# Part of the low-part work of layer one's gates on GpSimd, one gate kept in its PSUM bank, and the reserved bank also in layer two

## The chip, the cores and the metric

The kernel runs on one core of one Trainium2 chip. The metric is the device time of one execution in microseconds. The engines have short names in the profile: PE is TensorE (PEld its weight loads), DVE is VectorE, ACT is ScalarE, POOL is GpSimd, SP is SyncE. Times in the trace count from the start of the span.

## The reference, cut to what matters

A Fourier filter over the sequence comes first, then two feed-forward layers, all in float32:

```
y  = irfft(rfft(x) * (filt_r + 1j*filt_i))          # 2 x 3008 x 256 -> 6016 tokens x 256
h1 = y @ w_in                                       # 256 -> 2048
g1 = where(h1 > 0, h1, exp(min(h1, 0)) - 1)         # layer one: elu
z  = g1 @ w_out                                     # 2048 -> 256
h2 = z @ w2_in
out = (h2 * clip(h2 + 3, 0, 6) / 6) @ w2_out        # layer two
```

## The kernel before

Every matrix product of the two layers is done in three matmuls: operands are split into a high part (a rounded copy, made by ACT) and a low part (what is left, made by a subtraction). The three are weights-high by data-high, weights-low by data-high, weights-high by data-low (`mm3`, L88, L89 and L90). So the third matmul of each triple, L90, is the first to need the low part of the data.

The work of interest is that of **the groups**. The last four token blocks of layer one and all twelve of layer two are worked on in pairs, a pair being a round; layer one has two rounds, layer two six, and a round has eight groups, one for each two tiles of the hidden dimension. That makes 16 groups of layer one and 48 of layer two. A group takes a two-by-two block product with seven products instead of eight (`prod`, numbered 1 to 7, three matmuls each), which yields four hidden tiles, the keys (0,0), (1,1), (1,0) and (0,1). Of each hidden tile a gate value is made (`relu`, `exp`, `gate`), split (`high` on ACT at L674, `low` on DVE at L679), and multiplied with the output weights in the next group (`second`, two halves of three matmuls for each key). A group is thus 7 x 3 + 4 x 2 x 3 = 45 matmuls.

The order of the instructions on every engine is the order of the program's text. `elu_group` writes it out for layer one's groups and for the first group of layer two, `group` for the others. In them `old` is the group before, whose gates are finished and used, and `g` is the present one. In a layer-one group PE does prod 1, second (0,0), prod 2, 6, 5, second (1,1), prod 7, second (1,0), the first half of second (0,1), prod 4, the second half of second (0,1), prod 3. In the first group of layer two prod 2 stands ahead of second (0,0).

The gates of layer one need a minimum with zero, an exponential, and one scalar-tensor-tensor instruction on DVE (L666) that reads the exponential and the hidden tile h. For (0,0) h lies in a PSUM bank, for (1,0) too; for (1,1) and (0,1) it is a sum in SBUF (`add`, L634). Before, all four gates are written to SBUF, over the exponential.

At four places of a group, `slot(0)` to `slot(3)`, other work is put in: splits of the next round's operands (`x_high` L559 on ACT, `x_low` L564 on DVE; in groups 4 to 7 of a round `x_low` stands in `slot(1)`), the conversion of layer two's weights in small steps on ACT and DVE, and loads. POOL issues three kinds of loads in this stretch: `s0_load` (L384) and `s_load` (L389), the summed weights, and `w_load` (L457), layer two's weights. Each waits in POOL's queue until the buffer it fills is free. POOL has no arithmetic in these groups before.

PSUM has eight banks. Seven are handed out in turn (`bank()`, pool `ps`), one is reserved (`lone()`, pool `ps1`). A round keeps four banks for its outputs. A group takes three more for its products, a, b and c: prod 1, 6, 7 and 4 write to a, prod 2 to b, prod 5 and 3 to c. In layer one b is the reserved bank, and holds prod 1's result (copied by ACT, L750) before prod 2 is added to it; in layer two all three come from the seven.

Of the kernel before, what the change touches and what calls it, by code (L numbers as in the profile page):

```python
# [12 lines left out]
AF = mybir.ActivationFunctionType  # L13
ALU = mybir.AluOpType
# [28 lines left out]
def _f32(t):  # L43
    return t.bitcast(F32)
# [3 lines left out]
def fft_conv_moe_moe2(ctx, tc, xp, fq, sg, cs1, cs1t, cs2, ci2, ci1, ident, w1i, w1o, w2i, w2o, out):  # L48
    nc = tc.nc
# [11 lines left out]
    def name(s):  # L61
        uid[0] += 1
        return f"{s}_{uid[0]}"
# [4 lines left out]
    def t2(shape, dt=F32):  # L68
        return p2.tile(shape, dt, tag="t2", name=name("t2"))

    def bank():
        return ps.tile([P, 512], F32, tag="ps", name=name("ps"))

    def lone():
        return ps1.tile([P, 512], F32, tag="lone", name=name("lone"))
# [25 lines left out]
    def halves_of(t, k=2):  # L101
        return t.rearrange("p (a b) -> p a b", a=k)
# [4 lines left out]
    def like(t, n):  # L107
        return t[:, :n] if n == 512 else halves_of(t[:, :n])
# [171 lines left out]
    stt = nc.vector.scalar_tensor_tensor  # L280
# [9 lines left out]
    def w_words(layer, f):  # L290
        raw = raws.pop((layer, f))
        low, high = raw[:, :, 0], raw[:, :, 1]
        v, e, r = t2([P, 512]), t2([P, 512], U32), t2([P, 512])
        ahead[layer, f] = v, r
        nc.scalar.activation(v, _f32(high), AF.Abs)
        yield
        nc.vector.tensor_scalar_max(v, v, LEAST)
        nc.vector.tensor_scalar(
            e, v.bitcast(U32), 3, 0x3FFFFFFF, op0=ALU.logical_shift_left, op1=ALU.bitwise_and
        )  # L300
        yield
        stt(out=v.bitcast(U32), in0=high, scalar=0xC0000000, in1=e, op0=ALU.bitwise_and, op1=ALU.bitwise_or)
        yield
        nc.vector.tensor_scalar(e, v.bitcast(U32), 0xFF800000, None, op0=ALU.bitwise_and)
        yield
        stt(out=r, in0=low, scalar=2.0**-52, in1=_f32(e), op0=ALU.mult, op1=ALU.mult)
        yield
# [262 lines left out]
    def prod(l, p, q, m, acc, start):  # L570
        n = WIDTHS[l, p]
        if m in (1, 2):
            w = wts[l, 2 * q][:, :, (m - 1) * P : m * P]
        elif m == 4:
            w = wts[l, 2 * q + 1][:, :, P : 2 * P]
        else:
            w = sums[l, q][:, :, {5: 0, 6: 1, 7: 2, 3: 3}[m], :]
        x = ops[l, p, m]
        mm3(acc[:, :n], w[:, 0], w[:, 1], pairs(x[:, 0, :n]), pairs(x[:, 1, :n]), start, True, True)
# [40 lines left out]
    class Group:  # L620
# [39 lines left out]
        def gate(self, key):  # L660
            h, r = self.source(key), like(self.g[key], self.n)
            del self.h[key]
            if self.l:
                stt(out=r, in0=r, scalar=6.0, in1=h, op0=ALU.min, op1=ALU.mult)  # L664
            else:
                stt(out=r, in0=r, scalar=-1.0, in1=h, op0=ALU.add, op1=ALU.max)  # L666

        def part(self, key):
            self.high(key)
# [1 line left out]

        def high(self, key):
            g, gh = self.g[key], t2([P, 512], F32R)
            nc.scalar.activation(gh[:, : self.n], g[:, : self.n], AF.Copy)  # L674
            self.g[key] = g, gh

        def low(self, key):
            (g, gh), gl, n = self.g[key], t2([P, 512], F32R), self.n
            nc.vector.tensor_tensor(out=gl[:, :n], in0=g[:, :n], in1=_f32(gh[:, :n]), op=ALU.subtract)  # L679
            self.g[key] = gh, gl  # L680

        def second(self, key, d=(0, 1)):
# [7 lines left out]
    def group(l, p, q, old, first, beside):  # L690

        def slot(i):
            for fn in beside[i]:
                fn()

        g = Group(l, p, q)
        a, b, c = bank(), bank() if l else lone(), bank()
        if l == 0 or (old and old.l == 0):
            return elu_group(g, a, b, c, old, first, slot)
        prod(l, p, q, 1, a, True)  # L700
        m1 = g.copy(a)
        prod(l, p, q, 2, b, True)
        g.add((0, 0), m1, b)
        old.part((1, 0))
        old.relu((0, 1))
        old.gate((0, 1))
        old.second((0, 0))
        g.relu((0, 0))
        g.gate((0, 0))
        slot(0)  # L710
        prod(l, p, q, 6, a, False)
        u2 = g.copy(a)
        old.part((0, 1))
        slot(1)
        prod(l, p, q, 5, c, True)
        g.part((0, 0))
        slot(2)
        old.second((1, 1))
        prod(l, p, q, 7, a, False)
        u3 = g.copy(a)  # L720
        g.add((1, 1), u3, c)
        old.second((1, 0))
        old.finish(0)
        g.relu((1, 1))
        g.gate((1, 1))
        slot(3)
        old.second((0, 1), (0,))
        prod(l, p, q, 4, a, False)
        g.h[1, 0] = a
        g.relu((1, 0))  # L730
        if not g.last:
            g.gate((1, 0))
        old.second((0, 1), (1,))
        old.finish(1)
        if g.last:
            g.u2, g.c = u2, c
            return g
        g.part((1, 1))
        prod(l, p, q, 3, c, False)
        g.add((0, 1), u2, c)  # L740
        return g
# [268 lines left out]
    with tc.manual_schedule():  # L1010
# [27 lines left out]
        for step in PROLOGUE.split():  # L1038
            what, h, g = step[:-2], int(step[-2]), int(step[-1])
# [68 lines left out]
        n = place[0] = NU  # L1108
        for l, p in ROUNDS:
            for q in range(GROUPS):  # L1110
                old = group(l, p, q, old, [rest(NU + i) for i in range(3)], pre[n : n + 4])
                n += 4
# [98 lines left out]
```

## Time and profile before

| what | value |
|---|---|
| time, median of 3 runs | 1054.93 us (1054.42 to 1055.36) |
| the profiled execution | 1063.18 us, of which the span is 1061.4 us |
| PE busy | 1048.8 us, 99% of the span |
| DVE busy | 886.1 us, 83% |
| ACT busy | 797.7 us, 75% |
| POOL busy | 202.7 us, 19% |
| granted clock of TensorE | full in every slice |

The profiled execution is 8.25 us longer than the median of the runs. A matmul of 512 columns stands in the trace with 0.38 us, while the next one starts 0.22 us after it, since matmuls overlap; a stall of PE therefore shows as a longer step between two starts, and in the idle time before a weight load (PEld), with the engine whose semaphore ended it.

### The profile page before, as it was taken

The numbers are of one execution on the slowest core, as the hardware profiler recorded it, in microseconds if no ns is written. First come the engines' busy times: TensorE is split into PE (matmuls) and PEld (weight loads), VectorE is DVE, ScalarE is ACT, GpSimd is POOL, SyncE is SP. The second block draws the span as 40 slices with busy tenths as digits, with TensorE's granted clock in tenths as the row PEclk, the third lists the DMA queues.
The fourth block names the chain that finished last, engine by engine and source line by source line (L and its number), as shares of the span: only waits on it lengthen the run. The fifth ranks groups of instructions, "written<-read, shape, count | busy, mean of one in ns | idle before, by whom it ended". The sixth has DMA issues, their size and how long they took to land.

```text
span 1061.4 us, 14383 instructions
## 1 busy us (share of the span) xinstructions
PE 1048.8 (99%) x5022; PEld 918.7 (87%) x5022; DVE 886.1 (83%) x1427; ACT 797.7 (75%) x1437; POOL 202.7 (19%) x218
## 2 busy tenths in 40 slices
PE   9999999999999999999999999999999999999998
PEld 7688888888889989988888888888888888888998
DVE  2899999898886799889989978888888888888776
ACT  2478888897767888877877867777777777777766
POOL 1720000444546745300021100010010010000000
PEclk9999999999999999999999999999999999999999
DMA  9785100374645454610365710100100100100100
GB/s 278 246 263 198 50 16 1 106 222 151 196 135 178 153 193 152 213 55 6 133 236 161 231 73 21 60 1 21 60 14 27 40 18 18 41 1 1 40 1 35
DMA packets 57944, 107.31 MB, mean 101 GB/s; under 512 B 5008, under 2 KB 33680, under 8 KB 57872
## 3 DMA queue, kind: packets, MB, share of 16 engines
q1 hardware_dynamic: 52144, 88.21, 25.3%
q0 software_dynamic: 4896, 17.83, 5.4%
q8 instruction: 39, 0.64, 0.3%
q10 hardware_dynamic: 832, 0.36, 0.1%
q14 instruction: 33, 0.27, 0.1%
HBM read 69.42 MB, written 36.96 MB: 100 GB/s over the span
## 4 chain that ended last, share of the span: by engine, by line
PE 82%; ACT 7%; DVE 7%; issue 2%; DMA 2%; POOL 1%; SPq 0%; DVEq 0%; ACTq 0%; POOLq 0%
PE ps L90 24%; PE ps L88 24%; PE ps L89 24%; PE ps L158 2%; PE lone L88 1%; PE lone L90 1%; PE lone L89 1%; PE ps L245 1%; DVE t L85 1%; ACT t L84 1%; DMA scr<-t 1%; POOL t L217 1%; DVE t L679 1%; PE ps L202 1%; DVE t L634 1%
## 5 line engine op out<-in xcount | busy, mean ns | idle before, releaser
L88 PE MATMUL ps<-t,w 128*128 128x512 f32 (+1 forms) x1120 | 421.2, 376 | 2.3 <-DVE t L634 1.3
L90 PE MATMUL ps<-t,w 128*128 128x512 f32 (+1 forms) x1120 | 420.2, 375 | 0.7 <-DVE t L85 0.6
L89 PE MATMUL ps<-t,w 128*128 128x512 f32 (+1 forms) x1120 | 419.6, 375 | 0.2 <-DVE w L316 0.2
L88 PEld LDWEIGHTS ps<-t,w 128*128 128x128 f32 x1120 | 211.7, 189 | 29.4 <-DVE t L498 1.9
L90 PEld LDWEIGHTS ps<-t,w 128*128 128x128 f32 x1120 | 211.6, 189 | 28.4 <-DVE t L679 2.2
L89 PEld LDWEIGHTS ps<-t,w 128*128 128x128 f32 x1120 | 211.7, 189 | 25.9 <-DVE w L316 1.6
L679 DVE TENSOR_TENSOR t<-t,t 128x512 fp32r<-128x512 f32 (+1 forms) x256 | 175.7, 701 | 24.1 <-ACT t L674 22.5
L674 ACT ACTIVATE t<-t 128x512 fp32r<-128x512 f32 (+1 forms) x256 | 154.0, 616 | 6.1 <-DVE t L664 5.7
L628 ACT ACTIVATE t<-ps 128x512 f32<-128x512 f32 (+1 forms) x176 | 103.2, 586 | 64.9 <-PE ps L90 63.3
L634 DVE TENSOR_TENSOR t<-ps,t 128x512 f32<-128x512 f32 (+1 forms) x176 | 118.1, 679 | 14.2 <-ACT t L628 13.0
L664 DVE SCALAR_TENSOR_TENSOR t<-t,t 128x512 f32<-128x512 f32 (+1 forms) x144 | 97.6, 705 | 33.3 <-ACT t L648 32.7
L648 ACT ACTIVATE t<-t,three 128x512 f32<-128x512 f32 (+1 forms) x144 | 97.2, 707 | 37.3 <-DVE t L634 36.6
L495 ACT ACTIVATE t<-ps 128x512 f32<-128x512 f32 (+1 forms) x128 | 74.1, 579 | 30.1 <-PE ps L90 28.1
L84 ACT ACTIVATE t<-t 128x512 fp32r<-128x512 f32 (+2 forms) x108 | 66.2, 618 | 22.5 <-POOL t L217 20.0
L496 ACT ACTIVATE t<-t 128x512 f32<-128x512 f32 (+1 forms) x128 | 79.3, 619 | 4.1
L85 DVE TENSOR_TENSOR t<-t,t 128x512 fp32r<-128x512 f32 (+2 forms) x96 | 73.3, 769 | 10.6 <-ACT t L84 10.4
L548 POOL TENSOR_TENSOR t<-t,t 128x512 f32<-128x512 f32 (+1 forms) x12 | 16.2, 1351 | 286.0 <-DVE t L634 257.0
L498 DVE SCALAR_TENSOR_TENSOR ps<-t,ps 128x512 f32<-128x512 f32 (+1 forms) x76 | 50.4, 663 | 23.0 <-ACT t L496 22.5
L88 PE MATMUL ps<-t,t 128*128 128x512 f32 (+1 forms) x160 | 60.2, 376 | 0.6 <-DVE t L634 0.6
L89 PE MATMUL ps<-t,t 128*128 128x512 f32 (+1 forms) x160 | 60.1, 376 | 0.0
L90 PE MATMUL ps<-t,t 128*128 128x512 f32 (+1 forms) x160 | 60.1, 376 | 0.0
L85 DVE TENSOR_TENSOR t<-ps,t 128x512 fp32r<-128x512 f32 (+1 forms) x76 | 49.9, 656 | 0.1
(115 smaller groups left out, 1520.6 us busy)
## 6 DMA issues: line engine op xcount, KB each, us to landing
t<-in_fq SPq DMA_DIRECT2D x24, 512.0 KB, 6.2
scrw<-t SPq DMA_DIRECT2D x16, 512.0 KB, 2.8
w<-scrw POOLq DMA_DIRECT2D x16, 512.0 KB, 5.0
t<-in_xp SPq DMA_DIRECT2D x16, 384.0 KB, 6.0
scr<-t SPq DMA_DIRECT2D x24, 256.0 KB, 3.0
t<-scr SPq DMA_DIRECT2D x16, 384.0 KB, 5.2
scrx<-t SPq DMA_DIRECT2D x10, 512.0 KB, 3.3
t<-scr POOLq DMA_DIRECT2D x10, 512.0 KB, 6.1
```

The source lines that it names most:

```text
L84: nc.scalar.activation(hi, src, AF.Copy)
L85: eng.tensor_tensor(out=lo, in0=src, in1=_f32(hi), op=ALU.subtract)
L88: nc.tensor.matmul(acc, wh, xh, start=start, stop=False, skip_group_check=more)
L89: nc.tensor.matmul(acc, wl, xh, start=False, stop=False, skip_group_check=more)
L90: nc.tensor.matmul(acc, wh, xl, start=False, stop=stop, skip_group_check=more)
L496: nc.scalar.activation(t[:, :n], t[:, :n], AF.Exp, scale=-1.0)
L628: nc.scalar.activation(like(t, self.n), got(bank_, self.n), AF.Copy)
L634: nc.vector.tensor_tensor(out=like(self.h[key], n), in0=got(bank_, n), in1=like(u, n), op=ALU.add)
L648: nc.scalar.activation(like(r, n), h, AF.Relu, bias=three)
L664: stt(out=r, in0=r, scalar=6.0, in1=h, op0=ALU.min, op1=ALU.mult)
L674: nc.scalar.activation(gh[:, : self.n], g[:, : self.n], AF.Copy)
L679: nc.vector.tensor_tensor(out=gl[:, :n], in0=g[:, :n], in1=_f32(gh[:, :n]), op=ALU.subtract)
```

## The change

In layer one's groups the low parts of keys (0,0) and (0,1) are made by POOL and no longer by DVE. The gate of key (1,0) is written back to the PSUM bank that holds h, in place, and its high and low parts are then made from the bank, which is held until the low part is done. In layer two's groups b is the reserved bank, as in layer one. High and low parts are written through the same view as the gate, which changes nothing for blocks of 512 columns.

```
         def gate(self, key):
             h, r = self.source(key), like(self.g[key], self.n)
             del self.h[key]
             if self.l:
                 stt(out=r, in0=r, scalar=6.0, in1=h, op0=ALU.min, op1=ALU.mult)
+                self.g[key] = r
             else:
-                stt(out=r, in0=r, scalar=-1.0, in1=h, op0=ALU.add, op1=ALU.max)
+                g = h if key == (1, 0) else r
+                stt(out=g, in0=r, scalar=-1.0, in1=h, op0=ALU.add, op1=ALU.max)
+                self.g[key] = g
...
         def high(self, key):
             g, gh = self.g[key], t2([P, 512], F32R)
-            nc.scalar.activation(gh[:, : self.n], g[:, : self.n], AF.Copy)
+            nc.scalar.activation(like(gh, self.n), g, AF.Copy)
             self.g[key] = g, gh
 
         def low(self, key):
             (g, gh), gl, n = self.g[key], t2([P, 512], F32R), self.n
-            nc.vector.tensor_tensor(out=gl[:, :n], in0=g[:, :n], in1=_f32(gh[:, :n]), op=ALU.subtract)
+            eng = nc.gpsimd if not self.l and key in ((0, 0), (0, 1)) else nc.vector
+            eng.tensor_tensor(out=like(gl, n), in0=g, in1=_f32(like(gh, n)), op=ALU.subtract)
             self.g[key] = gh, gl
...
         g = Group(l, p, q)
-        a, b, c = bank(), bank() if l else lone(), bank()
+        a, b, c = bank(), lone(), bank()
```

## Rows read from the trace of the kernel before

**Rows 1.** Windows: length, busy of five engines (instructions), clock, DMA; layer one's groups, layer two's

```profile
436.00:517.00 81.00, 80.25 (x371) 68.96 (x370) 72.45 (x130) 63.43 (x118) 6.69 (x10) 1.00 0.27 89
597.00:677.00 80.00, 79.89 (x370) 69.64 (x370) 65.88 (x106) 57.96 (x100) 1.58 (x3) 1.00 0.22 72
```

**Rows 2.** Waits of PE's weight loads, 436 to 600 us: total, times, longest

```profile
PEld ps L88 <- DVE t L634: 2.8, 2, 1.7
PEld ps L90 <- DVE t L679: 2.0, 7, 0.5
PEld lone L88 <- ACT lone L750: 0.7, 2, 0.4
```

**Rows 3.** Timeline: start, duration, instruction, idle before; one late weight load, matmuls around it

```profile
482.09 0.19 PEld L90 LDWEIGHTS ps<-t,w 128*128 128x128 f32 x1 [0.22 <-DVE t L679]
...
482.11 0.47 PE L90 MATMUL ps<-t,w 128*128 128x512 f32 x1
482.42 0.38 PE L88 MATMUL ps<-t,w 128*128 128x512 f32 x1
```

**Rows 4.** Timeline of PE's weight loads at two starts of a round of layer two

```profile
595.64 0.19 PEld L88 LDWEIGHTS ps<-t,w 128*128 128x128 f32 x1 [1.71 <-DVE t L634]
...
673.72 0.19 PEld L88 LDWEIGHTS ps<-t,w 128*128 128x128 f32 x1 [0.51 <-DVE t L664]
```

**Rows 5.** Timeline of ACT in layer one's thirteenth group, which starts at 555.51

```profile
555.51 0.58 ACT L750 ACTIVATE lone<-ps 128x512 f32<-128x512 f32 x1 [1.32 <-PE ps L90]
...
558.11 0.60 ACT L628 ACTIVATE t<-ps 128x512 f32<-128x512 f32 x1
...
560.28 0.61 ACT L674 ACTIVATE t<-t 128x512 fp32r<-128x512 f32 x1
...
561.27 0.62 ACT L674 ACTIVATE t<-t 128x512 fp32r<-128x512 f32 x1
```

**Rows 6.** Timeline of DVE in the same group

```profile
561.01 0.68 DVE L679 TENSOR_TENSOR t<-t,t 128x512 fp32r<-128x512 f32 x1
561.61 0.68 DVE L564 TENSOR_TENSOR t<-t,t 128x512 fp32r<-128x512 f32 x1
```

**Rows 7.** Timeline of PE's weight loads in the same group

```profile
561.79 0.19 PEld L89 LDWEIGHTS ps<-t,w 128*128 128x128 f32 x1
562.01 0.19 PEld L90 LDWEIGHTS ps<-t,w 128*128 128x128 f32 x1
...
565.25 0.19 PEld L90 LDWEIGHTS ps<-t,w 128*128 128x128 f32 x1
```

**Rows 8.** Line 85, the same subtraction elsewhere: ns min/median/max, first and last start, shapes

```profile
L85 DVE TENSOR_TENSOR t<-t,t x96: 657/685/1774, 58.4 to 393.7; 128x512 fp32r<-128x512 f32 x76, 96x512 fp32r<-96x512 f32 x16, 128x448 fp32r<-128x448 f32 x4
...
L85 DVE TENSOR_TENSOR t<-ps,t x76: 610/677/727, 221.4 to 439.4; 128x512 fp32r<-128x512 f32 x44, 128x448 fp32r<-128x448 f32 x32
...
L85 POOL TENSOR_TENSOR t<-t,t x12: 1274/1279/1289, 235.8 to 309.6; 128x512 fp32r<-128x512 f32 x12
```

**Rows 9.** Timeline of POOL and DVE where their instructions overlap, two places

```profile
840.82 1.28 POOL L548 TENSOR_TENSOR t<-t,t 128x512 f32<-128x512 f32 x1 [47.11 <-DVE t L634]
...
840.91 1.74 DVE L679 TENSOR_TENSOR t<-t,t 128x512 fp32r<-128x512 f32 x1
...
428.53 0.69 DVE L564 TENSOR_TENSOR t<-t,t 128x512 fp32r<-128x512 f32 x1
...
428.58 1.78 POOL L330 TENSOR_TENSOR t<-t,t 128x512 fp32r<-128x512 f32 x1
```

**Rows 10.** Timeline of ACT and POOL: a high part, and POOL's low part of it

```profile
253.94 0.63 ACT L84 ACTIVATE t<-t 128x512 fp32r<-128x512 f32 x1
...
254.70 1.28 POOL L85 TENSOR_TENSOR t<-t,t 128x512 fp32r<-128x512 f32 x1 [1.96 <-issue]
```

**Rows 11.** Timeline of POOL's loads in layer one's groups

```profile
508.33 0.53 POOL L384 DMA_DIRECT2D t<-scr  x1 [44.19 <-PE lone L90]
...
581.68 0.53 POOL L457 DMA_DIRECT2D w<-scrw  x1 [7.24 <-PE ps L90]
```

More of the change, by code (lines that the diff above doesn't have):

```diff
@@ L664, in gate @@
                 stt(out=r, in0=r, scalar=6.0, in1=h, op0=ALU.min, op1=ALU.mult)
+                self.g[key] = r
             else:
-                stt(out=r, in0=r, scalar=-1.0, in1=h, op0=ALU.add, op1=ALU.max)
+                g = h if key == (1, 0) else r
+                stt(out=g, in0=r, scalar=-1.0, in1=h, op0=ALU.add, op1=ALU.max)
+                self.g[key] = g
         def part(self, key):
@@ L673, in high @@
             g, gh = self.g[key], t2([P, 512], F32R)
-            nc.scalar.activation(gh[:, : self.n], g[:, : self.n], AF.Copy)
+            nc.scalar.activation(like(gh, self.n), g, AF.Copy)
             self.g[key] = g, gh
@@ L678, in low @@
             (g, gh), gl, n = self.g[key], t2([P, 512], F32R), self.n
-            nc.vector.tensor_tensor(out=gl[:, :n], in0=g[:, :n], in1=_f32(gh[:, :n]), op=ALU.subtract)
+            eng = nc.gpsimd if not self.l and key in ((0, 0), (0, 1)) else nc.vector
+            eng.tensor_tensor(out=like(gl, n), in0=g, in1=_f32(like(gh, n)), op=ALU.subtract)
             self.g[key] = gh, gl
@@ L696, in group @@
         g = Group(l, p, q)
-        a, b, c = bank(), bank() if l else lone(), bank()
+        a, b, c = bank(), lone(), bank()
         if l == 0 or (old and old.l == 0):
```

## The prediction

> **What bounds the kernel now.** The page comes first: TensorE is busy for nearly the whole span (the table above), so no other engine can be worth more than the gaps in TensorE's stream. The windows come second, because the edits touch two stages [rows 1]. In both the granted clock is 1.00, TensorE's upper level, and TensorE starts a matmul about every 0.216 us (45 matmuls, a group, take 9.72 us); but VectorE is busy 72.45 of 81 us in layer one's groups and 65.88 of 80 us in layer two's. So layer one's groups run with VectorE close behind TensorE, and layer two's have room.
>
> The third view is the waits of TensorE's weight loads from 436 to 600 us [rows 2]: 2.0 us in seven waits for a low part (L679), 2.8 us in two for a sum (L634), 0.7 us in two for the copy into the reserved bank. A weight load normally runs ahead of its matmul, so a wait costs less than it shows. The late load at 482.09 waited 0.22 us, and the matmul behind it started 0.31 us after the one before, 0.09 us over the step of 0.216 [rows 3]. I take off 0.13 us for each wait. That gives 2.0 - 7 x 0.13 = 1.1 us for the low parts; for the two sums 2.8 - 0.26 = 2.5 us; for the copy 0.44 us. Together 4.1 us, of which one sum, 1.71 - 0.13 = 1.58 us at 595.64, stands at the border of the layers [rows 4]; the other 2.5 us lie inside the layer-one groups. After that, the only one of size is 0.51 - 0.13 = 0.38 us at 673.72. The whole prize is therefore 4.5 us, 0.4%.
>
> **The reserved bank in layer two.** At 595.64 prod 2 of the first layer-two group wants its bank and gets it only when the last layer-one sum has been read (L634); at 673.72 prod 2 wants the bank that the gate of (1,0) still reads (L664) [rows 4]. The reserved bank was read out by the gate of (0,0) a good five us before, so both waits go: -1.58 and -0.38, -1.96 us. Late next would be prod 6, which waits for the copy of prod 1; nine matmuls, 1.9 us, now stand between, and the copy takes 0.6. The other bound is 0, if another wait takes its place. I take -1.96.
>
> **The gate in its bank.** The same number of instructions, with one operand moved. From a bank, the low-part subtraction on VectorE has a median of 677 ns (with narrower shapes among them), from SBUF 685 [rows 8]: 0. On ScalarE a copy from a bank takes 0.60 and one from SBUF 0.61 [rows 5]; at most 0.03 us are won for what follows. The bank is held some 3 us longer, into the next group. Four output banks, the old a, the new a and c are seven, so there is one for everybody: 0. If the count were wrong, the loss would be like that at 595.64, 1.6 us a group. [...]
>
> **The low part of (0,0) on GpSimd.** The instruction takes 1.28 us there against 0.685 [rows 8]. It is due at the next group's start: its high part ends at 561.89, the load that needs it stands at 565.25 [rows 5, 7]. GpSimd can end at about 563.6 even behind the other low part. It is hidden under prods 4 and 3 and the second products, with 1.6 us left: 0. Without this cover each further 1.28 us on GpSimd would eat it up.
>
> **The low part of (0,1) on GpSimd.** This is the step that decides. Follow the thirteenth group. ScalarE starts the copy of prod 1 at its end, 555.51; prod 6 ends twelve matmuls later (12 x 0.216 = 2.59), and its copy starts at 558.11. From there ScalarE runs without a pause to the high part of (0,1), 560.28 to 560.89 [rows 5]. So this time is tied to TensorE, not to VectorE, and relieving VectorE can't bring it forward. On VectorE the low part ran from 561.01 to 561.69 [rows 6], and the load that needs it stood at 562.01 [rows 7]. GpSimd starts some 0.08 to 0.13 us after ScalarE (254.57 to 254.70) [rows 10] and takes 1.28: 562.25 to 562.30, less 0.03 for the copy from the bank. With 0.05 us for the semaphore the load starts some 0.3 us late, and costs 0.3 + 0.03 - 0.13 = 0.2 us. No group escapes this but the one that spans the border, where layer two's first key has no exponential.
>
> Three groups have two extra ScalarE instructions in slot(0). Five instructions already fill the 2.60 us from 555.51 to 558.11 [rows 5], so the second delays all by a step of about 0.5 us: 0.65 us each, 2.0 us.
>
> In ten groups (one of those three among them) VectorE has another two-input or conversion instruction right behind the gate of (0,0). It would start in the slot that the low part leaves, at 561.01, while GpSimd starts between 560.97 and 561.02. Here the rows show a lock. With GpSimd first by 0.09 us, VectorE's instruction with two SBUF inputs took 1.74 instead of 0.69; with VectorE first by 0.05 us, GpSimd's took 1.78 instead of 1.28 [rows 9]. If GpSimd is first, the cost to TensorE stays 0.2. If VectorE is first, GpSimd ends 561.01 + 1.83 = 562.84 and the load is 0.88 late: 0.77. Which wins can't be read from a margin of 0.04 us; I take GpSimd in two of three, 0.39 us, for nine groups 3.5 us.
>
> [...]
>
> **The relief of VectorE.** It gives up 32 x 0.6 = 19 us of issue slots (561.01 to 561.61 is one [rows 6]). Where it was late that could win the other sum, 2.5 - 1.58 = 0.9 us, in a group with three conversion instructions ahead of it. But these can now be held by GpSimd's two low parts: +1.06 against -0.6 for the first. I take 0.9 to 1.4, so 1.4, bounds 0.9 and 2.2. The 0.44 us of late copies stay at 0.5; the exponential of (1,1) behind VectorE's minimum can be held as well (bound 1.0).
>
> **Sum.** Inside the groups: 2.0 + 3.5 + 0.6 (three quiet groups at 0.2) + 1.4 + 0.5 = 8.0 us instead of 2.5, +5.5; with -1.96 it is +3.5. The profiled execution, 1063.18 (1061.4 of span and 1.78 around it), would be 1066.7; the median stands 8.25 us below, and I carry the difference over: 1054.93 + 3.5 = 1058.4 us. Its own bounds: all races to GpSimd, and 0.9: 2.0 + 1.8 + 0.6 + 0.9 + 0.5 = 5.8, +1.3, 1056.3; all to VectorE, 2.0 + 6.9 + 0.6 + 2.2 + 1.0 = 12.7, +8.2, 1063.2.
>
> **The rivals.** *No change:* every group loses the 0.2 and hardly more, ScalarE's extra steps are absorbed because it is no longer held by VectorE, and the sum and copies come in time: 16 x 0.2 = 3.2 instead of 2.5, with -1.96 it is -1.3, 1053.7, and up to the forecast's lower bound, 1056.3; in the middle 1055.0. For it speaks that ScalarE often waits for VectorE here; against it, that the chain from prod 6 starts at TensorE.
>
> *Faster:* the low part of (0,1) comes before its load. It decides at a high part that ends 0.2 us sooner, about 5.15 us after the copy of prod 1 starts (here 5.38). Then all gaps close: -4.1 - 0.38 = -4.5, 1050.4. For it: seven of the eleven waits name VectorE's low parts [rows 2]. Against it: the chain above.
>
> *GpSimd's queue:* its loads wait in order, 44.19 us for a buffer at 508.33, and 7.24 us for a matmul at 581.68 [rows 11]. A low part queued behind such a wait comes late. Against it: GpSimd reaches these loads groups ahead of their place in the program today, because it has nothing else to do; now it meets them in order, when the buffers are free. If not, the low part of (0,0) behind a second such load, nine matmuls later (581.68 + 1.94 + 0.53 = 584.15), ends at 585.4, some 0.8 us after TensorE wants it there, in each of six groups: with the forecast's other terms 1058.4 + 5 = 1063.4.
>
> **Chances.** Forecast 0.52, no change 0.30, faster 0.13, queue 0.05. A change of 0.2%, 2.1 us, is about what a measurement here can tell from none. Faster 0.13; within 0.2% the 0.30 and 0.05 of the forecast's lower end, 0.35; slower 0.52. The range from 1053.5 to 1062.8 leaves out the faster case, the queue, and the forecast's last tip, not quite 2 in 10.
>
> **What would show it.** Right: no idle time at prod 2 at the two borders; weight loads of L90 waiting for GpSimd's L679 once a group, 0.3 us or more; VectorE instructions of 1.7 us, or GpSimd's of 1.8, in slot(1). Wrong: these waits gone, or named by a DMA, or loads waiting for a new bank.

## The result, and the profile after

The changed kernel takes 1062.82 us (median of 4 runs, 1062.14 to 1062.88), the kernel before 1055.13 us in the same comparison (4 runs, 1054.42 to 1055.36). It is 7.7 us slower; the ratio is 1.0073, with a 95% interval from 1.0055 to 1.0090. Forecast were +3.5 us and a range up to 1062.8: the direction was right, the size less than half of what came, and the time lies just past the range.

The two profiled executions can't be compared by their spans, since the profile of before is one of its longer executions (three of 68 later runs of before lay near 1063 us too). That of before (1061.4 us) reached its first layer-one group at 438.19 us, that of the changed kernel (1060.3 us) at 429.58, a difference of 8.6 us ahead of the groups, in a part which the change doesn't touch. From there to the end before took 623.19 us and the changed kernel 630.76: +7.57 us, which agrees with the medians.

The windows of the changed kernel, with the columns of [rows 1]; its groups start 8.6 us earlier:

```profile
436.00:517.00 81.00, 77.04 (x346) 64.42 (x346) 72.41 (x112) 61.39 (x115) 23.90 (x20) 1.00 0.20 65
...
597.00:677.00 80.00, 79.81 (x370) 69.46 (x370) 67.56 (x107) 59.66 (x104) 8.14 (x14) 1.00 0.37 130
```

In the window in layer one's groups TensorE does 346 matmuls where it did 371. VectorE is busy for as long as before (72.41 against 72.45 us) with fewer instructions, 112 against 130. The windows hold different parts of the work, so here is the same stretch of it in both, from the first group's copy of prod 1 on, with 714 matmuls recorded: VectorE was busy for 140.96 us with 250 instructions in before (438.19 to 594.41), and is for 143.98 us with 218 now (429.58 to 594.44). That is the first sign: 32 instructions were taken from it, and it is no less busy. In layer two the matmuls run as before (370 in either window).

The waits of TensorE's weight loads from 429 to 604 us, in the changed kernel (total, times, longest), beside [rows 2]:

```profile
PEld ps L90 <- POOL t L683: 7.8, 15, 0.8
PEld ps L88 <- DVE t L634: 4.4, 3, 2.0
PEld lone L88 <- ACT lone L754: 2.4, 4, 0.9
PEld ps L90 <- DVE t L683: 0.6, 1, 0.6
```

L683 is the low part (L679 before), L634 the sum, L754 ScalarE's copy of prod 1 into the reserved bank; below they are called low parts, sums and copies. With the prediction's 0.13 us taken off each wait, the low parts on GpSimd cost 7.8 - 15 x 0.13 = 5.85 us, the sums 4.4 - 3 x 0.13 = 4.0, the copies 2.4 - 4 x 0.13 = 1.9, and a low part on VectorE 0.5. By their places all 15 waits for GpSimd are for the low part of (0,1). That is 12.2 us; in before it was 4.1 us and 0.38 at the second border. The difference, 7.7 us, is the whole result.

At the borders the waits are gone. TensorE's weight loads of prod 2 there, which answer to [rows 4]:

```profile
594.23 0.19 PEld L90 LDWEIGHTS ps<-t,w 128*128 128x128 f32 x1
594.44 0.19 PEld L88 LDWEIGHTS lone<-t,w 128*128 128x128 f32 x1
...
672.40 0.19 PEld L90 LDWEIGHTS ps<-t,w 128*128 128x128 f32 x1
672.61 0.19 PEld L88 LDWEIGHTS lone<-t,w 128*128 128x128 f32 x1
```

What holds VectorE is seen best in the fifteenth group, which starts at 573.70. Its timeline, GpSimd first, then VectorE, ScalarE and TensorE's weight loads:

```profile
579.10 1.27 POOL L683 TENSOR_TENSOR t<-t,t 128x512 fp32r<-128x512 f32 x1 [4.61 <-ACT t L677]
...
580.34 1.72 POOL L683 TENSOR_TENSOR t<-t,t 128x512 fp32r<-128x512 f32 x1
...
579.13 1.79 DVE L375 TENSOR_TENSOR t<-t,t 128x512 fp32r<-128x512 f32 x1
580.85 1.76 DVE L564 TENSOR_TENSOR t<-t,t 128x512 fp32r<-128x512 f32 x1
582.53 0.68 DVE L634 TENSOR_TENSOR t<-ps,t 128x512 f32<-128x512 f32 x1
583.24 0.43 DVE L637 TENSOR_SCALAR t<-t 128x512 f32<-128x512 f32 x1
...
583.76 0.64 ACT L654 ACTIVATE t<-t 128x512 f32<-128x512 f32 x1 [3.74 <-DVE t L637]
...
580.43 0.19 PEld L90 LDWEIGHTS ps<-t,w 128*128 128x128 f32 x1 [0.62 <-POOL t L683]
...
583.26 0.19 PEld L88 LDWEIGHTS ps<-t,t 128*128 128x128 f32 x1 [1.46 <-DVE t L634]
```

GpSimd starts the low part of (0,1) 0.03 us before VectorE's next instruction, which takes 1.79 us. It ends 0.55 us after GpSimd's, about the 0.6 us of a slot, so by these rows it ran only when GpSimd was done. GpSimd's second low part, that of (0,0), is in its turn held by it and shows 1.72; VectorE's second instruction is held by that one, and takes 1.76 us. The sum (L634) starts at 582.53, and prod 3, which wants its bank, waits 1.46 us. In the first group, where GpSimd makes only the low part of (0,0), that one holds VectorE's minimum (L637). GpSimd, VectorE and the weight load of the next group's prod 2:

```profile
435.65 1.27 POOL L683 TENSOR_TENSOR t<-t,t 128x512 fp32r<-128x512 f32 x1 [5.96 <-ACT t L677]
...
435.82 1.39 DVE L637 TENSOR_SCALAR t<-t 128x512 f32<-128x512 f32 x1
...
439.33 0.19 PEld L88 LDWEIGHTS lone<-t,w 128*128 128x128 f32 x1 [0.94 <-ACT lone L754]
```

The minimum takes 1.39 us instead of 0.43; the exponential behind it, the next copy on ScalarE and with it prod 2 come late. That an instruction of GpSimd and one of VectorE hold each other up in this way is called the lock below, as in the prediction. Over all groups, line 683 (ns min/median/max):

```profile
L683 POOL TENSOR_TENSOR t<-t,t x32: 1263/1366/1809, 435.7 to 600.2; 128x512 fp32r<-128x512 f32 x32
...
L683 DVE TENSOR_TENSOR t<-ps,t x16: 679/692/693, 442.5 to 599.9; 128x512 fp32r<-128x512 f32 x16
```

### The profile page after: what moved, and what is told of

Its sections match the earlier page's. It is cut to its first block, busy times and chain, and to the rows that moved or that the text cites. A ratio compares the mean times of both kernels' runs of the same rounds, so it can differ in the third digit from the quotient of the medians.

```text
span 1060.3 us, 14429 instructions
## 1 busy us (share of the span) xinstructions
PE 1043.7 (98%) x5022; PEld 910.6 (86%) x5022; DVE 888.8 (84%) x1395; ACT 797.1 (75%) x1437; POOL 248.5 (23%) x250
## 4 chain that ended last, share of the span: by engine, by line
PE 80%; ACT 8%; DVE 7%; issue 3%; POOL 1%; DVEq 0%; POOLq 0%; ACTq 0%
PE ps L90 23%; PE ps L88 23%; PE ps L89 23%; PE lone L88 2%; PE lone L89 2%; PE lone L90 2%; PE ps L245 2%; PE ps L158 1%; DVE t L85 1%; ACT t L84 1%; ACT t L658 1%; ACT t L677 1%; POOL t L217 1%; ACT t L495 1%; ACT t L650 1%
## 5 line engine op out<-in xcount | busy, mean ns | idle before, releaser
L90 PE MATMUL ps<-t,w 128*128 128x512 f32 (+1 forms) x1072 | 403.3, 376 | 2.9 <-POOL t L683 2.0
L88 PE MATMUL ps<-t,w 128*128 128x512 f32 (+1 forms) x1072 | 402.9, 376 | 0.9 <-DVE t L498 0.8
L89 PE MATMUL ps<-t,w 128*128 128x512 f32 (+1 forms) x1072 | 401.6, 375 | 0.2 <-DVE w L316 0.2
L90 PEld LDWEIGHTS ps<-t,w 128*128 128x128 f32 x1072 | 202.5, 189 | 33.4 <-POOL t L683 7.8
L88 PEld LDWEIGHTS ps<-t,w 128*128 128x128 f32 x1072 | 202.6, 189 | 25.1 <-DVE t L498 1.9
L89 PEld LDWEIGHTS ps<-t,w 128*128 128x128 f32 x1072 | 202.6, 189 | 25.0 <-DVE w L316 1.7
L683 DVE TENSOR_TENSOR t<-t,t 128x512 fp32r<-128x512 f32 (+1 forms) x208 | 142.5, 702 | 19.5 <-ACT t L677 17.9
L677 ACT ACTIVATE t<-t 128x512 fp32r<-128x512 f32 (+1 forms) x240 | 144.2, 616 | 7.4 <-DVE t L664 6.9
L634 DVE TENSOR_TENSOR t<-ps,t 128x512 f32<-128x512 f32 (+1 forms) x128 | 86.7, 677 | 13.5 <-ACT t L628 13.0
L683 POOL TENSOR_TENSOR t<-t,t 128x512 fp32r<-128x512 f32 x32 | 45.6, 1434 | 114.9 <-ACT t L677 102.0
L90 PE MATMUL ps<-t,t 128*128 128x512 f32 (+1 forms) x160 | 60.1, 376 | 0.0
```

What stands on the lines that cost most here:

```text
L88: nc.tensor.matmul(acc, wh, xh, start=start, stop=False, skip_group_check=more)
L89: nc.tensor.matmul(acc, wl, xh, start=False, stop=False, skip_group_check=more)
L90: nc.tensor.matmul(acc, wh, xl, start=False, stop=stop, skip_group_check=more)
L634: nc.vector.tensor_tensor(out=like(self.h[key], n), in0=got(bank_, n), in1=like(u, n), op=ALU.add)
L677: nc.scalar.activation(like(gh, self.n), g, AF.Copy)
L683: eng.tensor_tensor(out=like(gl, n), in0=g, in1=_f32(like(gh, n)), op=ALU.subtract)
```

## The experiments

Theory: the loss has two causes of like size, both GpSimd's. The low part of (0,1) comes too late for its weight load; and GpSimd's instructions keep VectorE out, the low part of (0,0) above all, so that sums and copies come late. Rivals: the bank that is held longer; late results alone; the lock alone. All times are differences to the kernel before in the same comparison, whose median was 1055.01, 1055.19 and 1055.28 us in the three.

**The bank edit alone (e1).** Before, with one line:

```
-        a, b, c = bank(), bank() if l else lone(), bank()
+        a, b, c = bank(), lone(), bank()
```

> Before, with the reserved bank for prod 2 in layer two and nothing else. My theory: the two waits of prod 2 at the borders of rounds go (1.58 and 0.38 us) and nothing takes their place, -1.9 us against before. Rival: another wait takes their place (the weight load of L90 in the first layer-two group waited 0.46 us in the changed kernel), -1 us or less.

Measured: 1053.07 us, -1.94; ratio 0.9975 (0.9959 to 0.9992). The term of -1.96 is borne out; that the two agree to 0.02 us is luck, since the interval reaches from -4.3 to -0.8 us. The waits at the borders are gone from the trace.

**GpSimd's low parts alone (e2).** The changed kernel with the gate in SBUF and the old b:

```
-                g = h if key == (1, 0) else r
+                g = r
...
-        a, b, c = bank(), lone(), bank()
+        a, b, c = bank(), bank() if l else lone(), bank()
```

> The two low parts on GpSimd; the gate of (1,0) in SBUF and layer two's b from the seven banks, as before. Theory: all of the loss is GpSimd's, and it is larger than the changed kernel's by the two border waits that come back: +9.5 us against before, and a little more where the low part of (1,0), now from SBUF, meets GpSimd's lock. Rival: the loss is the bank's, held longer by the gate in it; then this is -1 to +1 us.

Measured: 1064.79 us, +9.78; ratio 1.0083 (1.0058 to 1.0109). With the bank edit's 1.94 taken off, 7.84, it is the changed kernel's loss of 7.7 us. So the loss comes with GpSimd's low parts.

**The gate in its bank alone (e3).** The changed kernel with all low parts on VectorE and the old b.

```
-            eng = nc.gpsimd if not self.l and key in ((0, 0), (0, 1)) else nc.vector
+            eng = nc.vector
...
-        a, b, c = bank(), lone(), bank()
+        a, b, c = bank(), bank() if l else lone(), bank()
```

> Before, with the gate of (1,0) in its bank and nothing else; low parts on VectorE. Theory: no change, within 0.5 us. Rival (the bank is held too long): weight loads wait for a bank, +5 us or more.

Measured: 1054.41 us, -0.60; ratio 0.9990 (0.9975 to 1.0006): no change that the interval shows. TensorE's weight loads wait as in before (from 429 to 620 us 1.8 us for low parts, 2.7 for sums, 0.7 for copies, against [rows 2]); none waits for the bank that the gate holds.

**GpSimd busy for nothing (e4).** The changed kernel with all low parts on VectorE; both bank edits are kept. Behind two of the four low parts GpSimd adds high and low into a tile that is read by nobody.

```
-            eng = nc.gpsimd if not self.l and key in ((0, 0), (0, 1)) else nc.vector
+            eng = nc.vector
             eng.tensor_tensor(out=like(gl, n), in0=g, in1=_f32(like(gh, n)), op=ALU.subtract)
+            if not self.l and key in ((0, 0), (0, 1)):
+                nc.gpsimd.tensor_tensor(out=warm, in0=_f32(gh[:, :n]), in1=_f32(gl[:, :n]), op=ALU.add)
```

> The changed kernel with all low parts back on VectorE, while GpSimd, behind the same two low parts, adds the high and the low part into a tile that nobody reads: nothing waits for GpSimd's results any more, but it takes its lock as often. Theory of the lock: VectorE's next instructions still take 1.7 us, the sums and copies come late as in the changed kernel, and VectorE has its two low parts as well: +4 to +9 us against before. Rival, lateness of GpSimd's results alone: nobody waits for it, -2 us as with the reserved bank alone.

Measured: 1073.93 us, +18.92; ratio 1.0169 (1.0130 to 1.0208), twice what I expected at most. Against e7 below, which differs by nothing but GpSimd's 32 instructions, these cost 21 us, though no instruction of another engine waits for one of them. Two of VectorE's instructions, grouped by shape (count, busy us, mean ns), and TensorE's waits from 429 to 620 us:

```profile
L668 DVE SCALAR_TENSOR_TENSOR t<-t,t 128x512 f32<-128x512 f32 x31 | 30.6, 989 | 0.4 <-ACT t L654 0.2
L637 DVE TENSOR_SCALAR t<-t 128x512 f32<-128x512 f32 x32 | 19.3, 602 | 1.3
...
PEld ps L90 <- DVE t L683: 15.8, 31, 1.0
PEld ps L88 <- DVE t L634: 12.3, 16, 1.9
```

In e7 the same two groups have means of 685 and 427 ns. So the lock costs without any late result: here it falls on the gates (L668) and the minimum, and what follows on VectorE is late for TensorE. GpSimd's instructions start behind VectorE's low parts, so they meet other instructions than in the changed kernel; the run shows what the lock can do, and not how much of the changed kernel's loss it makes (e6 does). That it is worse than in the changed kernel I put down to VectorE's having the low parts as well; this is argued, not tried.

**One low part each (e5, e6).** The changed kernel with GpSimd making that of (0,1) alone, and that of (0,0) alone:

```
-            eng = nc.gpsimd if not self.l and key in ((0, 0), (0, 1)) else nc.vector
+            eng = nc.gpsimd if not self.l and key == (0, 1) else nc.vector      # e5
+            eng = nc.gpsimd if not self.l and key == (0, 0) else nc.vector      # e6
```

> The changed kernel with the low part of (0,0) back on VectorE; GpSimd makes that of (0,1) alone. Theory (late result for L90, about 6 us, and two locks in a row behind the gate of (0,0)): the late result stays, the second lock goes, so the waits for sums and copies fall from 6 to 2 or 3 us: +3 to +6 us against before. Rival (the locks hardly count, GpSimd's result is all of it): +7.5 us, as the changed kernel.

> The changed kernel with the low part of (0,1) back on VectorE; GpSimd makes that of (0,0) alone, which is due 1.5 us later. Theory: L90 waits as before (1 us), one lock a group is left, which can hold an operand split, a weight step or the minimum: waits for sums and copies 2 to 3 us; -1 to +2 us against before. Rival (the lock is what costs, wherever it falls): +4 us or more.

Measured: e5 1059.64 us, +4.45, ratio 1.0035 (1.0019 to 1.0050); e6 1057.94 us, +2.75, ratio 1.0014 (0.9993 to 1.0036; its ten runs span 1057.47 to 1058.54). e5 came as expected; e6 is above the +2 us that I expected at most, and below the rival's +4. Waits of TensorE's weight loads from 429 to 620 us, e5 and then e6:

```profile
PEld ps L90 <- POOL t L683: 9.0, 16, 1.6
PEld ps L88 <- DVE t L634: 1.8, 3, 1.0
PEld lone L88 <- ACT lone L754: 0.7, 2, 0.4
```

```profile
PEld ps L88 <- DVE t L634: 4.1, 3, 2.1
PEld ps L90 <- DVE t L683: 2.9, 9, 0.6
PEld lone L88 <- ACT lone L754: 2.5, 3, 0.9
```

This tells the two apart. With (0,1) alone, L90 waits for GpSimd sixteen times, fifteen in the changed kernel, while sums and copies wait hardly more than before. With (0,0) alone, no load waits for GpSimd, L90 waits 2.9 us for VectorE's low parts, and sums and copies wait as in the changed kernel (4.1 and 2.5 against 4.4 and 2.4). So the low part of (0,0), whose own result is never late, makes those waits. In e6's fifteenth group, GpSimd and VectorE:

```profile
576.33 1.45 POOL L683 TENSOR_TENSOR t<-t,t 128x512 fp32r<-128x512 f32 x1 [5.62 <-ACT t L677]
...
575.96 0.69 DVE L375 TENSOR_TENSOR t<-t,t 128x512 fp32r<-128x512 f32 x1
576.56 1.76 DVE L564 TENSOR_TENSOR t<-t,t 128x512 fp32r<-128x512 f32 x1
578.25 0.68 DVE L634 TENSOR_TENSOR t<-ps,t 128x512 f32<-128x512 f32 x1
```

In e5, VectorE's next instruction is ahead of GpSimd's in four of the ten groups where it has one ready at that moment. GpSimd's then takes 1.79 or 1.80 us, and L90 waits 0.88 to 1.60 us. GpSimd and VectorE in the thirteenth group:

```profile
557.40 1.79 POOL L683 TENSOR_TENSOR t<-t,t 128x512 fp32r<-128x512 f32 x1 [8.19 <-ACT t L677]
...
557.37 0.68 DVE L564 TENSOR_TENSOR t<-t,t 128x512 fp32r<-128x512 f32 x1
```

**No low part on GpSimd (e7).** Both bank edits, all low parts on VectorE.

```
-            eng = nc.gpsimd if not self.l and key in ((0, 0), (0, 1)) else nc.vector
+            eng = nc.vector
```

> The changed kernel with both low parts on VectorE: the gate in its bank and the reserved bank alone. Theory: the two add up, -1.9 and -0.6, so -2.2 to -2.8 us against before, faster than both kernels. Rival (the bank held longer hurts when both are done): -1 us or less.

Measured: 1052.79 us, -2.40; ratio 0.9971 (0.9954 to 0.9987), faster than both kernels. Waits from 429 to 620 us:

```profile
PEld ps L90 <- DVE t L683: 1.8, 7, 0.5
PEld ps L88 <- DVE t L634: 1.0, 1, 1.0
PEld lone L88 <- ACT lone L754: 0.7, 2, 0.4
```

Against it, (0,1) on GpSimd costs 6.85 us (e5), (0,0) 5.15 us (e6), both 10.0 us (1062.82, from the other comparison): two like parts that overlap by 2 us. The waits, less 0.13 us each, say the same. Over e7, (0,1) alone adds 6.1 us for L90, 0.5 for sums and nothing for copies; (0,0) alone 0.8, 2.8 and 1.7; both together 5.4, 3.1 and 1.4. So 1.5 of the 2 us of overlap lie in L90's waits, and 1.1 of these in its waits for GpSimd, 6.9 us in e5 against 5.85: e5 has four low parts that VectorE held, the changed kernel one.

**The high part of (0,1) earlier (e8).** The changed kernel with one instruction of ScalarE moved up by two places (negative part and exponential of (0,0)):

```
             old.high((1, 0))
+            old.high((0, 1))
         g.relu((0, 0))
         if old:
             old.low((1, 0))
-            old.high((0, 1))
```

> The changed kernel with the high part of (0,1) one place earlier on ScalarE, ahead of the negative part and exponential of (0,0), so that GpSimd can start its low part some 1.2 us sooner. Theory: the wait of L90, 6 us in the changed kernel, falls under 1 us; the gate of (0,0) comes 0.5 us later; the locks stay, so that 2 to 5 us of the waits for sums and copies stay: between 0 and +3 us against before. Rival (the locks alone make the loss, L90's waits are only where it shows): +5 us or more.

Measured: 1056.00 us, +0.81, ratio 1.0002 (0.9987 to 1.0018); 6.8 us less than the changed kernel. From 429 to 620 us:

```profile
PEld lone L88 <- ACT lone L754: 3.0, 4, 1.2
PEld ps L90 <- DVE t L683: 2.6, 7, 0.7
PEld ps L88 <- DVE t L634: 1.4, 2, 1.1
```

GpSimd's name is gone from L90's waits, as the theory said. What L90 still waits, 2.6 - 7 x 0.13 = 1.7 us, is for other low parts, on VectorE; I had expected less than 1 us.

**Better versions (e9, e10).** e9 is e7 with the move of e8, and VectorE's low part of (0,1) ahead of the gate of (0,0); e10 is e5 with the move of e8.

```
             old.low((1, 0))
+            old.low((0, 1))            # e9
         g.gate((0, 0))
-        if old:
-            old.low((0, 1))
```

> No low part on GpSimd; the gate in its bank, the reserved bank, the high part of (0,1) one place earlier on ScalarE, and its low part ahead of the gate of (0,0) on VectorE. Theory: L90's waits of 0.5 us that are left without GpSimd go too, the late sum of group 5 may come 0.5 us later, since the gate of (0,0) does: -2 to -3.5 us against before. Rival (the later gate of (0,0) sets off waits elsewhere): slower than the two banks alone, that is above -2 us.

> GpSimd makes the low part of (0,1) alone, with its high part one place earlier; (0,0) on VectorE; both bank edits. Theory (of the 7.6 us lost, (0,0)'s lock behind the sums and copies is one half and the late result of (0,1) the other): both are gone here, its lock falls while VectorE waits for the exponential of (0,0): -2 to -4 us against before. Rival (a two-input instruction of GpSimd costs in this stage wherever it stands): +1 us or more.

Measured: e9 1052.69 us, -2.59, ratio 0.9977 (0.9966 to 0.9987); e10 1052.71 us, -2.57, ratio 0.9974 (0.9965 to 0.9984). Neither can be told from e7, so e10's low part of (0,1) on GpSimd gains nothing that can be seen. Yet e10 shows that it can be free. Its thirteenth group, GpSimd and VectorE, and TensorE's largest waits from 429 to 620 us:

```profile
551.77 1.27 POOL L683 TENSOR_TENSOR t<-t,t 128x512 fp32r<-128x512 f32 x1 [7.92 <-ACT t L677]
...
551.14 0.69 DVE L683 TENSOR_TENSOR t<-ps,t 128x512 fp32r<-128x512 f32 x1
552.88 0.69 DVE L668 SCALAR_TENSOR_TENSOR t<-t,lone 128x512 f32<-128x512 f32 x1 [1.05 <-ACT t L658]
553.49 0.69 DVE L564 TENSOR_TENSOR t<-t,t 128x512 fp32r<-128x512 f32 x1
...
PEld ps L88 <- DVE t L634: 1.1, 1, 1.1
PEld lone L88 <- ACT lone L754: 0.9, 2, 0.6
```

GpSimd runs from 551.77 to 553.04, while VectorE reads a bank or waits for the exponential of (0,0). It is the same instruction that cost 6.85 us in e5.

## Why the prediction was too small

- **The reserved bank.** Right: -1.96 forecast, -1.94 measured (e1), where no wait takes the place of those at the borders.
- **The gate in its bank.** Right: 0 forecast, -0.6 within the interval (e3). VectorE's low part from the bank has a median of 692 ns [rows 8 had 677 and 685], and in e7 a mean of 689 against 685 from SBUF, 0.004 us more.
- **The low part of (0,1).** The size was right, its make-up only in part: 6.1 us forecast for L90's waits, 5.85 measured. Ten groups had an instruction of VectorE ready at that moment, as I had counted. In nine of them GpSimd started first, by 0.02 to 0.11 us, and took 1.26 to 1.28 us; in one VectorE was 0.03 us ahead, and GpSimd took 1.53. I had given VectorE a third. On the other hand, ScalarE's high part came late in six groups, where I had marked three (it ended 5.50 to 5.83 us after the copy of prod 1 starts). That these two errors nearly cancel is luck. The group at the border was let off rightly: the 0.5 us lost there are a wait for VectorE's low part of (1,0).
- **The low part of (0,0). This step failed.** I costed it at 0, since its own result has 1.6 us to spare. That is so: no load waits for it. But in this term I asked only when its result is due, and not whom the instruction keeps out while it runs. Alone it costs 5.15 us (e6 against e7), of which 4.5 are waits for sums and copies. It stands right behind the other low part, so in the fifteenth group, which has two instructions of VectorE after the gate of (0,0), each is held by one of GpSimd's (1.79 and 1.76 us instead of 0.69); in others it holds the minimum (1.39 us instead of 0.43 in the first).
- **The relief of VectorE, mis-sized for this reason.** Sums: 1.4 us forecast, bounds 0.9 and 2.2, measured 4.0. Late copies: 0.5 forecast, bound 1.0, measured 1.9. There was no relief: VectorE gave up 32 slots of 0.6 us, 19 us, and was busy for 3 us more than before. The lock was in the sum only for one instruction a group; the second low part and the minimum (0.43 us, held to 1.39) stood in the bounds, where they belonged in the sum. The minimum is a tensor-scalar instruction with one input, and the trace of before has such a one slow beside GpSimd too: L298 took 1.38 us from 374.09, with GpSimd's L375 at work from 373.71 to 375.19, against a median of 0.43. The upper bound of 1063.2 comes near the measured time by another way: it lets VectorE win every race, 9.5 us of waits for L90, where 5.85 came.
- **The rivals.** No change and faster did not come: L90 waited for GpSimd in each of fifteen groups. Nor did the wait in GpSimd's queue: the low parts of (0,1) start 0.07 to 0.15 us after ScalarE's high part is done, so no load holds them. That the low part of (0,1) comes in time needed the move of e8.

With the two terms as measured, 5.85 + 4.0 + 1.9 + 0.5 - 2.5 - 1.96 = +7.8 us.

What stays open: why GpSimd starts first in nine of ten groups of the changed kernel and in six of ten of e5, with leads of some hundredths of a microsecond. By the waits about 1 us hangs on it, and no run controls it.

## What to carry to other kernels

Before moving an elementwise instruction from VectorE to GpSimd, look at what VectorE runs in the 1.3 us that it takes there. Here an instruction with two SBUF inputs took up to 1.79 us beside it instead of 0.69, and the minimum, a tensor-scalar one, up to 1.39 instead of 0.43: the move gave VectorE nothing (143.98 us busy against 140.96), and held up work that has nothing to do with the result. Count this for every instruction moved, also for those whose results have time. Place it where VectorE reads PSUM (its sums took 0.66 to 0.69 us beside GpSimd's) or waits, by making its input earlier if need be: one ScalarE instruction moved up turned +4.45 us into -2.57. Ask too whether there is a gain left: here the two bank edits without GpSimd (e7) are as fast.

## What the runs showed of the hardware that was not expected

GpSimd's 32 instructions whose results nobody uses cost 21 us of 1053 (e4 against e7), more than when TensorE waits for their results. A start 0.03 us sooner decided which of the two engines was held: VectorE by 1.1 us (579.10 against 579.13 in the changed kernel), or GpSimd by 0.5 (557.37 against 557.40 in e5). Two-input instructions of VectorE that read one operand from PSUM ran at 0.66 to 0.69 us beside GpSimd's, as the changed kernel's sums (0.67 to 0.69 without it).
